# Attention weights spread by transfers instead of matmuls, with a new order of loads

## The chip, the cores and the metric

The kernel runs on one core of one Trainium2 chip. The metric is the device time of one execution in microseconds (us). Three runs of the kernel before took 202.96, 203.83 and 204.58 us; the median, 203.83 us, is the time before.

## What is computed

One transformer layer on x of 2048 rows and 512 columns, in bf16. Attention has 32 heads of 16 columns, and each row attends to 8 rows: itself and the rows 2, 4, ... 14 before it. The feed-forward part (FFN) has 1376 columns and multiplies a ReLU gate with a second projection.

```
qkv = layernorm(x) @ wqkv                    # q, k, v: 32 heads x 16
idx = pos[:, None] - 2 * arange(8)           # 8 rows per position, masked below 0
attn = softmax(einsum("bhsd,bhswd->bhsw", q, k[idx]) * 16**-0.5)
o = einsum("bhsw,bhswd->bhsd", attn, v[idx])
h = x + o @ wo
g = layernorm(h) @ W_gate
out = h + (g * (g > 0) * (layernorm(h) @ W_up)) @ W_down
```

## The kernel before

The rows are worked on in four chunks of 512, numbered 0 to 3 (`tk`). The activations lie transposed: `xnT`, `qT`, `kT`, `vT`, `OT` and `hnT` have 512 columns of the model spread over 128 partitions and 4 slices, and the rows along the free dimension. A chunk passes through these stages, and the engines work on several chunks at a time:

- Layer norm of x. DVE makes the statistics (L419, L422), ACT the reciprocal root (L432, L436), DVE the normed rows (L454, tiles named `row`). PE transposes them (L483) and ACT or DVE copies them out (L499, L497); for two pairs of rows in chunk 3 and for most of h, the transpose is a transfer on SP's queue (L472).
- Projections q, k, v: 12 tiles of four matmuls (L524), each copied out by ACT (L532). In chunk 0 the first four tiles go in halves of 256 columns.
- Scores. DVE multiplies q with four shifted views of k at a time (L571, 128 x 4096 elements; four such products a chunk), PE sums over the columns of a head (L577), ACT takes the exponential (L593). The 8 weights of a head come in two halves (`hf`) of four, each a tile `ex` of 128 partitions: 4 weights x 32 heads. In chunk 0 DVE masks them (L596). PE sums the weights (L610), ACT makes the reciprocal (L613, L616). In chunks 1 to 3 DVE multiplies the weights with it (L625).
- Spreading. v has four partitions for each head, so each weight's 32 partitions are spread to 128. PE does this with four matmuls against a 0/1 matrix for each half (L638), and ACT copies the four results (L644) into a tile `ab` of 128 x 8 x 512 from the pool `big`.
- Sum over the 8 rows. DVE multiplies `ab` with eight shifted views of v (L659, four products a chunk), and sums by halving (L662, then L666 or L685, which writes `OT`). In chunks 0 to 2 the first halving is an accumulating transfer on POOL's queue (L691).
- Output projection on PE (L711; in chunk 0 the residual is added there too, L714), residual and sums on ACT (L720) or DVE (L722), then the layer norm of h (L400, L408, L429, L436, L454) and its transposes.
- FFN. Up and gate tiles on PE (L749), ACT copies (L753) and ReLU (L756), DVE's product `gT` (L769), the down projection on PE (L786), the residual on DVE (L797), the store on SP's queue (L801).

The order on each engine is written out. Every step is added to a planner with an engine, a duration, a latency and the buffers it takes; a list RANK gives each step its place; the planner walks through the queues of the engines, picks for each the step with the lowest rank, assigns buffers by the planned times, and the instructions are issued in the order of the planned starts. Loads have planned arrival times and no place in a queue: they are issued in `setup()`. On the chip each engine works in the issued order and waits for semaphores.

Eight completion counts serve the transfers that SP and ACT issue, in turn: each transfer waits before its issue until the eighth transfer before it has landed.

The start: the four tiles of x of chunk 0 are loaded in turn from SP and ACT, then four loads of the q and k weights, each a quarter of the rows of both, then x of chunk 1 on SP (L285). The v weights are held back until the first tile of x has landed (L299, L300), and x of chunks 2 and 3 until that of chunk 1 has (L301, L303). wo, the up, gate and down weights follow on SP. PE runs 44 matmuls on zeros meanwhile (L373), and 8 after each of the first two transposes (L381).

Of the kernel before, what the change touches and what calls it, by code (L numbers as in the profile page):

```python
# [18 lines left out]
    0, 1, 2, 3, 4, 5, 6, 7, 8, 9, 10, 11, 12, 13, 14, 15, 16, 18, 19, 24,  # L19
    26, 31, 32, 17, 20, 22, 23, 25, 29, 34, 35, 28, 33, 37, 39, 41, 45, 48, 21, 27,  # L20
    30, 36, 38, 42, 44, 46, 63, 74, 40, 56, 68, 49, 51, 54, 43, 60, 72, 53, 66, 65,
    77, 70, 83, 75, 80, 90, 92, 87, 114, 102, 110, 85, 105, 93, 104, 115, 125, 129, 78, 88,
    95, 99, 103, 183, 193, 202, 132, 143, 150, 156, 152, 106, 109, 116, 123, 119, 168, 181, 216, 220,
    224, 180, 188, 217, 223, 231, 187, 196, 226, 229, 234, 162, 172, 201, 205, 207, 237, 240, 239, 245,
    247, 251, 242, 248, 243, 246, 252, 256, 259, 263, 250, 254, 265, 266, 272, 278, 269, 276, 285, 275,
    283, 273, 280, 286, 318, 322, 292, 301, 304, 314, 313, 324, 341, 311, 325, 298, 303, 334, 338, 326,
    330, 346, 354, 360, 337, 355, 317, 353, 347, 358, 370, 329, 352, 340, 348, 332, 345, 294, 350, 356,
    361, 374, 343, 365, 372, 381, 351, 362, 413, 357, 368, 367, 386, 418, 400, 425, 460, 464, 417, 427,
    457, 467, 376, 434, 446, 466, 410, 429, 437, 668, 55, 61, 52, 57, 50, 58, 47, 59, 62, 64,
    67, 84, 73, 82, 86, 71, 81, 69, 79, 89, 166, 175, 122, 136, 111, 130, 137, 190, 91, 101,  # L30
    127, 173, 149, 179, 94, 96, 163, 213, 158, 170, 98, 107, 108, 167, 208, 197, 249, 257, 244, 235,
    255, 260, 264, 268, 274, 296, 279, 302, 309, 305, 310, 307, 287, 295, 290, 293, 300, 319, 328, 364,
    369, 315, 320, 359, 363, 335, 342, 380, 382, 327, 336, 373, 375, 389, 395, 387, 392, 396, 402, 393,
    399, 398, 401, 397, 403, 405, 409, 404, 407, 411, 412, 416, 419, 420, 423, 421, 428, 422, 426, 431,
    474, 482, 441, 443, 458, 463, 453, 468, 483, 438, 448, 436, 452, 442, 451, 450, 454, 456, 488, 492,
    479, 498, 455, 487, 491, 500, 507, 461, 493, 445, 459, 481, 485, 471, 475, 496, 511, 539, 524, 533,
    520, 535, 526, 530, 541, 514, 540, 484, 502, 543, 544, 556, 581, 589, 538, 552, 559, 562, 549, 554,
    584, 587, 529, 547, 560, 564, 113, 120, 100, 124, 76, 117, 97, 112, 128, 133, 140, 144, 142, 146,
    164, 145, 154, 148, 157, 161, 209, 230, 174, 186, 198, 200, 195, 215, 182, 184, 199, 228, 189, 211,
    169, 177, 178, 194, 232, 241, 271, 281, 185, 191, 261, 253, 284, 297, 289, 282, 308, 312, 321, 331,  # L40
    339, 344, 378, 366, 377, 371, 379, 383, 385, 394, 388, 391, 390, 430, 439, 470, 490, 424, 432, 473,
    476, 440, 447, 486, 489, 406, 415, 465, 477, 501, 518, 497, 504, 508, 512, 494, 499, 521, 525, 517,
    519, 516, 522, 503, 505, 527, 528, 532, 546, 534, 537, 536, 548, 531, 542, 579, 597, 566, 594, 585,
    601, 561, 580, 609, 599, 603, 588, 592, 571, 575, 577, 600, 605, 606, 610, 595, 623, 602, 611, 582,
    614, 627, 558, 576, 574, 578, 568, 572, 565, 567, 583, 621, 648, 639, 645, 636, 649, 591, 616, 652,
    624, 635, 628, 633, 640, 655, 663, 665, 667, 632, 654, 661, 711, 650, 656, 707, 710, 644, 657, 659,
    669, 126, 138, 118, 134, 131, 139, 121, 135, 141, 147, 155, 160, 151, 171, 159, 165, 153, 176, 203,
    236, 218, 225, 192, 204, 214, 219, 258, 291, 262, 270, 222, 233, 267, 277, 227, 238, 212, 221, 288,
    316, 206, 210, 306, 299, 323, 333, 384, 349, 408, 414, 433, 435, 444, 462, 449, 506, 510, 509, 513,
    515, 469, 495, 478, 472, 480, 563, 570, 586, 593, 523, 551, 557, 569, 573, 590, 596, 598, 545, 550,  # L50
    553, 555, 615, 622, 604, 607, 612, 619, 608, 613, 626, 629, 618, 620, 630, 631, 617, 625, 634, 637,
    638, 641, 646, 653, 643, 651, 642, 647, 691, 695, 681, 692, 694, 698, 688, 697, 700, 679, 687, 674,
    677, 670, 680, 666, 671, 690, 673, 675, 672, 682, 658, 662, 660, 678, 683, 684, 689, 664, 685, 699,
    702, 676, 693, 705, 701, 706, 704, 709, 686, 703, 708, 713, 715, 716, 718, 696, 714, 719, 720, 722,
    724, 731, 712, 726, 732, 734, 717, 725, 727, 730, 728, 733, 735, 737, 721, 723, 729, 736,
# [3 lines left out]
class Op:  # L59


    __slots__ = ("eng", "dur", "lat", "fn", "deps", "prio", "take", "use", "start", "done", "seq", "key")

    def __init__(self, eng, dur, fn, deps=(), prio=0.0, take=(), use=(), lat=0.0):
        self.eng, self.dur, self.fn, self.lat = eng, dur, fn, lat
        self.deps = [d for d in deps if d is not None]
        self.prio, self.take, self.use = prio, list(take), list(use)
        self.start = self.done = None
# [23 lines left out]
class Plan:  # L92
# [23 lines left out]
    def order(self):  # L116
# [14 lines left out]
        while left:  # L131
# [36 lines left out]
            op.start, op.done = t, t + op.dur + op.lat  # L168
            free[op.eng] = t + op.dur
# [18 lines left out]
def kernel(  # L188
# [20 lines left out]
    PADL = 16  # L209
    SCALE = DH ** -0.5  # L210
# [45 lines left out]
    big_s = slots(5, [P, W, CS], BF16, "big")  # L256
    gT_s = slots(7, [P, 2, CS], BF16, "gT")
    ex_s = slots(3, [P, CS], BF16, "ex")
    ln_s = slots(1, [P, CS], F32, "lnd")
# [18 lines left out]
    def setup():  # L278
# [4 lines left out]
        for dt in range(NT):  # L283
            (nc.scalar if dt % 2 else nc.sync).dma_start(wqk_sb[:, dt:dt + 1, :], w3_r[:, dt:dt + 1, 0:2 * D])
        nc.sync.dma_start(x_sm[:, BPC:2 * BPC, :], x_rows[:, BPC:2 * BPC, :])  # L285
# [13 lines left out]
        nc.gpsimd.tensor_copy(out=wv_sb[0:1, 0, 0:1], in_=x_sm[0:1, 0, 0:1])  # L299
        nc.sync.dma_start(wv_sb[:], w3_r[:, :, 2 * D:3 * D])  # L300
        nc.gpsimd.tensor_copy(out=x_sm[0:1, 2 * BPC, 0:1], in_=x_sm[0:1, BPC, 0:1])  # L301
        for tk in range(2, NCK):
# [4 lines left out]
        nc.sync.dma_start(wg_sb[:], B_W_gate.rearrange("(dt p) f -> p dt f", p=P))  # L307
        nc.sync.dma_start(
            wd_sb[:, 0:NFF, :], B_W_down[0:NFF * P, :].rearrange("(ft p) n -> p ft n", p=P))
        if FTAIL:  # L310
            nc.sync.dma_start(wd_sb[:FTAIL, NFF, :], B_W_down[NFF * P:F, :])

# [24 lines left out]
    NWARM, NFILL = 44, 8  # L337
    DMAT = (('h',2,0),('h',2,2),('x',3,0),('x',3,2),('h',3,0),('h',3,2),('h',1,0))

    EARLY = (1, 2, 3)  # L340

# [11 lines left out]
    MM, TP = 0.2165, 0.07  # L353
# [8 lines left out]
    def load(t):  # L362
        return add(None, "LD", 0.0, None, lat=t)

    xload = [[load(t) for t in (3.4, 3.4, 4.2, 4.2)]] + [[load(t)] * BPC for t in (9.5, 14.0, 15.5)]
    wload = {n: load(t) for n, t in
             (("q", 8.0), ("k", 8.0), ("v", 12.0), ("o", 17.5), ("u", 21.5), ("g", 25.5), ("d", 29.5))}
# [7 lines left out]
    fills = [add(("warm", 0), "PE", 5.7, f_warm, [], -500, take=[wb])]  # L375
# [9 lines left out]
    def layernorm(tk, src, dst_slots, pr, groups, on_act, residual=None):  # L385
# [7 lines left out]
        for grp in groups:  # L393
# [72 lines left out]
            for j0 in range(lo, hi, step):  # L466
                if (ln, tk, j0) in DMAT:
                    for j in range(j0, min(j0 + step, hi)):
                        xn, a = norm(j)

                        def f_td(j=j, xn=xn):
                            nc.sync.dma_start_transpose(out=dst.t[:, :, j * P:(j + 1) * P], in_=xn.t[:])  # L472

                        evs.append(add((ln + "td" + gk, tk), "SP", TDD, f_td, [a], pr, take=[dst], use=[xn], lat=TDL))
                    continue
# [31 lines left out]
    for tk in range(NCK):  # L507
# [9 lines left out]
        seq = [(c, t) for t in range(NT) for c in (0, 1)] + [(2, t) for t in range(NT)]  # L517
        for n, (c, t) in enumerate(seq):
# [38 lines left out]
        for hf in range(2):  # L557
# [26 lines left out]
            if tk in MERGE:  # L584
                scd = [add(("sc%d" % hf, tk), "PE", 4 * MM + SW, lambda p=prd: [f() for _, _, f in p],
                           [a for a, _, _ in prd], apr, take=[sc], use=[b for _, b, _ in prd], lat=PEL)]
            else:
                for a, pb, f in prd:
                    scd.append(add(("sc%d" % hf, tk), "PE", 2 * MM + SW, f, [a] + scd[-1:], apr,
                                   take=[sc], use=[pb], lat=PEL))  # L590
# [17 lines left out]
        def f_dn(exs=exs, dn=dn, tk=tk):  # L608
# [9 lines left out]
        b = add(("den", tk), "PE", 2 * MM, f_dn, exd, apr + 2, take=[dn], use=exs, lat=PEL)  # L618
# [11 lines left out]
        ab, abd = Buf(big_s), []  # L630
        for w0 in range(0, W, BCN):
            hf = w0 // 4
            bcs = [Buf(at_s) for _ in range(BCN)]
# [17 lines left out]
        for t in range(NT):  # L651
# [35 lines left out]
            for n, du in ((4, D20), (2, D10), (1, D2)):  # L687
                f = lambda n=n, mt=mt, f=f_a: f(n, mt)
                if n == 4 and (tk, t) in DACC:
# [3 lines left out]
                    m = add(("ta%d" % t, tk), "POOL", 1.5, f_da, [m], tpr, use=[mt], lat=DAL)  # L693
# [85 lines left out]
        for n, (j, c0, c1) in enumerate(parts):  # L779
# [20 lines left out]
            def f_os(j=j, c0=c0, c1=c1, ob=ob, tk=tk):  # L800
                nc.sync.dma_start(out_rows[:, tk * BPC + j, c0:c1], ob.t[:, c0:c1])  # L801
# [9 lines left out]
            add(("os%d" % n, tk), "SP", 0.15, f_os, [b], mb + 6, use=[ob], lat=2.0)  # L811
# [42 lines left out]
```

## Time and profile before

| | |
|---|---|
| median of three runs | 203.83 us (202.96 to 204.58) |
| span of the profiled execution (first to last instruction) | 200.7 us |
| that execution's own time | not listed by the page; the median lies 3.1 us above the span |
| PE busy | 193.4 us (96%) |
| DVE busy | 153.3 us (76%) |
| ACT busy | 121.8 us (61%) |
| transfers | 18.81 MB, mean 94 GB/s |
| first projection, first FFN tile, last down projection ends | 7.96, 65.22, 197.17 us |

Busy times are sums over the instructions of an engine. The strip of 40 digits divides the span into equal slices of 5 us and gives the busy share of each in tenths. A line of the waits names who waited, for whom, the sum in us, how often, and the longest. A line of the chain gives the start, the length and the work; "issue" is time in which the engine waited for nothing the profile shows. A line of the timeline gives start and length; the bracket at its end says how long the engine stood idle before it and what ended that. A line of the groups gives the busy time, the mean of one instruction in ns and the idle time before them. A line of the transfers gives their number, the size of each and the median time from issue to landing.

### The profile page before, as it was taken

How to read it: one execution, taken by the hardware profiler on the slowest of the kernel's cores; microseconds unless marked ns; L12 is line 12 of the kernel's file. 1: busy time of each engine (PE TensorE's matmuls, PEld its weight loads, DVE VectorE, ACT ScalarE, POOL GpSimd, SP SyncE). 2: the span in 40 equal slices, each digit the busy share in tenths (PEclk: the TensorE clock that was granted, in tenths of full speed). 3: DMA queues.
4: the chain of work that ended last, by engine and by line, in shares of the span. 5: the costliest groups of instructions: out<-in, count | busy, mean ns of one | idle time of the engine just before them, and what ended most of it. 6: DMA issues, size and time to landing. Idle time of an engine off the chain costs nothing.

```text
span 200.7 us, 2938 instructions
## 1 busy us (share of the span) xinstructions
PE 193.4 (96%) x1095; PEld 96.2 (48%) x1115; DVE 153.3 (76%) x239; ACT 121.8 (61%) x256; POOL 12.7 (6%) x28
## 2 busy tenths in 40 slices
PE   8999999989999999999999999999999999999992
PEld 8776445445445344444444444444444444444451
DVE  6989998989999999999996868799967412022313
ACT  3576798747899965887436779701566631277400
POOL 4000000410000013100131000000000000000000
PEclk9999999999999999999999999999999999999999
DMA  6989933994000009920399400131010050200103
GB/s 204 322 245 409 388 119 66 170 201 87 3 0 0 3 0 183 195 40 3 57 178 193 124 3 0 29 75 52 3 52 0 0 104 3 78 0 0 52 0 105
DMA packets 17676, 18.81 MB, mean 94 GB/s; under 512 B 8352, under 2 KB 14464, under 8 KB 17664
## 3 DMA queue, kind: packets, MB, share of 16 engines
q1 hardware_dynamic: 15360, 11.57, 18.5%
q0 software_dynamic: 1728, 6.29, 16.6%
q10 hardware_dynamic: 576, 0.79, 1.2%
q8 instruction: 8, 0.13, 0.3%
q14 instruction: 4, 0.03, 0.0%
HBM read 8.42 MB, written 2.10 MB: 52 GB/s over the span
## 4 chain that ended last, share of the span: by engine, by line
PE 67%; DVE 16%; DMA 6%; ACT 5%; issue 2%; SPq 1%; ACTq 0%
PE bank L749 29%; PE bank L524 15%; PE bank L786 14%; DVE big L659 6%; PE bank L711 5%; DMA quad<-row 5%; DVE big L571 3%; DVE gT L769 2%; DMA x_sm<-in_A_x_dram 1%; SPq L472 1%; PE bank L483 1%; DVE x_sm L722 1%; DVE big L662 1%; DVE row L454 1%; PE bank L577 1%
## 5 line engine op out<-in xcount | busy, mean ns | idle before, releaser
L749 PE MATMUL bank<-quad,wu_sb 128*128 128x512 bf16 (+1 forms) x172 | 42.4, 379 | 0.4
L749 PE MATMUL bank<-quad,wg_sb 128*128 128x512 bf16 (+1 forms) x173 | 42.0, 379 | 0.4 <-DMA quad<-row 0.3
L756 ACT ACTIVATE gr<-bank 128x512 bf16<-128x512 f32 (+1 forms) x44 | 25.3, 616 | 24.7 <-PE bank L749 22.9
L786 PE MATMUL bank<-wd_sb,gT 128*128 128x512 bf16 (+2 forms) x183 | 39.8, 366 | 0.2
L753 ACT CAST up_sb<-bank 128x512 bf16<-128x512 f32 (+1 forms) x44 | 25.0, 600 | 21.0 <-PE bank L749 17.3
L571 DVE TENSOR_TENSOR big<-quad,kT 128x4096 bf16<-128x4096 bf16 x16 | 36.2, 2284 | 0.2
L659 DVE TENSOR_TENSOR big<-big,vT 128x4096 bf16<-128x4096 bf16 x16 | 35.9, 2281 | 0.0
L769 DVE TENSOR_TENSOR gT<-gr,up_sb 128x1024 bf16<-128x1024 bf16 (+1 forms) x24 | 15.3, 642 | 24.0 <-ACT up_sb L753 14.4
L524 PE MATMUL bank<-quad,wqk_sb 128*128 128x512 bf16 (+1 forms) x139 | 29.9, 355 | 1.0 <-DMA quad<-row 0.8
L786 PEld LDWEIGHTS <-gT 128*128 128x128 bf16 (+1 forms) x187 | 18.1, 98 | 19.7 <-issue 0.4
L749 PEld LDWEIGHTS <-wg_sb 128*128 128x128 bf16 (+1 forms) x176 | 17.3, 100 | 21.2 <-issue 0.9
L749 PEld LDWEIGHTS <-wu_sb 128*128 128x128 bf16 (+1 forms) x176 | 17.5, 100 | 20.6 <-issue 0.7
L524 PEld LDWEIGHTS <-wqk_sb 128*128 128x128 bf16 x144 | 15.6, 114 | 12.8 <-issue 2.3
L797 DVE TENSOR_TENSOR row<-x_sm,bank 128x512 bf16<-128x512 bf16 (+1 forms) x17 | 10.6, 649 | 10.4 <-PE bank L786 10.4
L644 ACT CAST big<-bank 128x512 bf16<-128x512 f32 x32 | 17.8, 635 | 0.4 <-PE bank L638 0.2
L662 DVE TENSOR_TENSOR big<-big 128x1024 bf16<-128x1024 bf16 (+2 forms) x24 | 16.8, 728 | 0.1
L691 POOL DMA_DIRECT2D big<-big x12 | 10.5, 873 | 88.1 <-DVE big L659 59.9
L524 PE MATMUL bank<-quad,wv_sb 128*128 128x512 bf16 x62 | 15.6, 380 | 0.2
L711 PE MATMUL bank<-wo_sb,quad 128*128 128x512 bf16 x62 | 15.2, 379 | 0.2
L454 DVE TENSOR_SCALAR row<-x_sm,mv,rs 128x512 bf16<-128x512 bf16 x32 | 11.4, 407 | 3.7 <-ACT rs L436 3.1
L532 ACT CAST quad<-bank 128x512 bf16<-128x512 f32 x16 | 9.5, 612 | 4.6 <-PE bank L524 4.6
L499 ACT COPY quad<-bank 128x1024 bf16<-128x1024 bf16 (+1 forms) x9 | 8.0, 929 | 6.0 <-PE bank L483 6.0
(68 smaller groups left out, 147.2 us busy)
## 6 DMA issues: line engine op xcount, KB each, us to landing
big<-big POOLq DMA_DIRECT2D x12, 512.0 KB, 5.6
out_dram<-row SPq DMA_DIRECT2D x15, 128.0 KB, 1.8
x_sm<-in_A_x_dram SPq DMA_DIRECT2D x3, 512.0 KB, 5.5
wu_sb<-in_B_W_up_dram SPq DMA_DIRECT2D x1, 1376.0 KB, 8.6
wg_sb<-in_B_W_gate_dram SPq DMA_DIRECT2D x1, 1376.0 KB, 11.6
wd_sb<-in_B_W_down_dram SPq DMA_DIRECT2D x1, 1280.0 KB, 14.9
wqk_sb<-in_A_wqkv_dram ACTq DMA_DIRECT2D x2, 256.0 KB, 5.0
wqk_sb<-in_A_wqkv_dram SPq DMA_DIRECT2D x2, 256.0 KB, 5.2
```

Of the source, the lines that this page charges most:

```text
L454: V.tensor_scalar(out=xn.t[:], in0=x, scalar1=mv.t[:, j, 0:1], scalar2=rs.t[:, j:j + 1], op0=ALU.add if residual else ALU.subtract, op1=AL ...
L524: nc.tensor.matmul(mm.t[:, lo:hi], lhsT=wv_sb[:, dt, t:D:NT] if c == 2 else wqk_sb[:, dt, c * D + t:(c + 1) * D:NT], rhs=xnT.t[:, dt, lo:h ...
L571: V.tensor_tensor(out=pb.t[:].rearrange("p (t w) s -> p t w s", t=2), in0=q4, in1=k4, op=ALU.mult)
L644: nc.scalar.copy(out=ab.t[:, w, :], in_=bc.t[:])
L659: V.tensor_tensor(out=mt.t[:], in0=ab.t[:], in1=v8, op=ALU.mult)
L662: V.tensor_tensor(out=mt.t[:, 0:n, :], in0=mt.t[:, 0:n, :], in1=mt.t[:, n:2 * n, :], op=ALU.add)
L711: nc.tensor.matmul(od.t[:], lhsT=OT.t[:, t, j * P:(j + 1) * P], rhs=wo_sb[:, t, :], start=(t == 0), stop=(t == NT - 1 and tk not in RPE))
L749: nc.tensor.matmul(mm.t[:fs, :], lhsT=w_sb[:, dt, ft * P: ft * P + fs], rhs=hnT.t[:, dt, :], start=(dt == 0), stop=(dt == NT - 1))
L753: nc.scalar.copy(out=ub.t[:fs, i, :], in_=um.t[:fs, :])
L756: nc.scalar.activation(out=gr.t[:fs, i, :], in_=gm.t[:fs, :], func=ACT.Relu)
L769: V.tensor_tensor(out=gt.t[:fs, 0:n, :], in0=gr.t[:fs, 0:n, :], in1=ub.t[:fs, 0:n, :], op=ALU.mult)
L786: nc.tensor.matmul(od.t[:, c0:c1], lhsT=gts[ft].t[:fs, ft % 2, j * P:(j + 1) * P], rhs=wd_sb[:fs, ft, c0:c1], start=(ft == 0), stop=(ft == ...
```

## The change

- `ab` gets a buffer of its own, and the pool `big` has four instead of five. All spreading matmuls L638 and copies L644 go. In their place SP issues, for each half, four transfers within SBUF, one for each weight: 32 partitions of `ex` are read four times each and written to the 128 partitions of `ab[:, w, :]`, 128 KB each, 32 in all.
- The q weights are loaded first (two loads, on SP and ACT), then the k weights (two), then x of chunk 1 in two halves, one on SP and one on ACT, ahead of ACT's table load. The v weights wait for the first q load instead of the first x tile. In chunk 0 the projections go in the order q, k, v instead of q and k in turn.
- The loads of the gate and down weights become steps of the planner. In SP's order they stand where they stood.
- 42 warm-up matmuls instead of 44, and 4 instead of 8 after each of the two transposes.
- The last of the 17 stores in the planner's list is issued by ACT instead of SP.
- The planner models a queue of transfers (`dq`), some of its durations change, and RANK is a new list, so the order changes on every engine. On DVE, chunk 0's first normed row stands ahead of the third L419; three L419 of chunk 2 stand ahead of chunk 1's normed rows; five instead of four products L571 stand between chunk 0's last `OT` slice and the normed rows of h; chunk 1's first product with v stands after two instead of four products of later scores.
- Three switches are added that are off (`PRE`, `DEN1`) or change no instruction.

```
-    big_s = slots(5, [P, W, CS], BF16, "big")
+    NAB = 1
+    big_s = slots(5 - NAB, [P, W, CS], BF16, "big")
+    ab_s = slots(NAB, [P, W, CS], BF16, "ab") if NAB else big_s
...
-        for dt in range(NT):
-            (nc.scalar if dt % 2 else nc.sync).dma_start(wqk_sb[:, dt:dt + 1, :], w3_r[:, dt:dt + 1, 0:2 * D])
-        nc.sync.dma_start(x_sm[:, BPC:2 * BPC, :], x_rows[:, BPC:2 * BPC, :])
+        for c in range(2):
+            for h in range(2):
+                (nc.scalar if h else nc.sync).dma_start(
+                    wqk_sb[:, 2 * h:2 * h + 2, c * D:(c + 1) * D], w3_r[:, 2 * h:2 * h + 2, c * D:(c + 1) * D])
+        for h in range(2):
+            j = BPC + 2 * h
+            (nc.scalar if h else nc.sync).dma_start(x_sm[:, j:j + 2, :], x_rows[:, j:j + 2, :])
         nc.scalar.preload_act_table_set("natural_log_exp_and_others")
...
-        nc.gpsimd.tensor_copy(out=wv_sb[0:1, 0, 0:1], in_=x_sm[0:1, 0, 0:1])
+        nc.gpsimd.tensor_copy(out=wv_sb[0:1, 0, 0:1], in_=wqk_sb[0:1, 0, 0:1])
         nc.sync.dma_start(wv_sb[:], w3_r[:, :, 2 * D:3 * D])
...
-    NWARM, NFILL = 44, 8
+    NWARM, NFILL = 42, 4
...
+    BCD = tuple((k, h) for k in range(4) for h in range(2))
+    DMI = 0.42
...
+        if tk == 0:
+            seq = [(c, t) for c in range(3) for t in range(NT)]
...
-        ab, abd = Buf(big_s), []
+        ab, abd = Buf(ab_s), []
         for w0 in range(0, W, BCN):
             hf = w0 // 4
+            if (tk, hf) in BCD:
+                def f_bd(w0=w0, ab=ab, ex=exs[hf]):
+                    for w in range(w0, w0 + 4):
+                        r = w % 4 * HB
+                        nc.sync.dma_start(ab.t[:, w, :], ex.t[r:r + HB, :].unsqueeze(1).to_broadcast([HB, 4, CS]))
+
+                abd.append(add(("bd%d" % hf, tk), "SP", 4 * DMI, f_bd, [exd[hf]], apr + 1, take=[ab],
+                               use=[exs[hf]], lat=0.7, dq=(0.2, 1.54 - 3 * DMI)))
+                continue
...
-            def f_os(j=j, c0=c0, c1=c1, ob=ob, tk=tk):
-                nc.sync.dma_start(out_rows[:, tk * BPC + j, c0:c1], ob.t[:, c0:c1])
+            last = tk == NCK - 1 and n == len(parts) - 1
+
+            def f_os(j=j, c0=c0, c1=c1, ob=ob, tk=tk, q=nc.scalar if last else nc.sync):
+                q.dma_start(out_rows[:, tk * BPC + j, c0:c1], ob.t[:, c0:c1])
```

## Prediction

> **What bounds the kernel now.** I read the busy times first, then who waited for whom, then the chain of work that ended last, and last the timeline of the start.
>
> ```profile
> PE 193.4 (96%) x1095; PEld 96.2 (48%) x1115; DVE 153.3 (76%) x239; ACT 121.8 (61%) x256; POOL 12.7 (6%) x28
> ...
> PE   8999999989999999999999999999999999999992
> ...
> DVE  6989998989999999999996868799967412022313
> ```
>
> ```profile
> PE bank L373 <- DVE warm L287: 1.0, 1, 1.0
> PE bank L524 <- DMA quad<-row: 0.8, 1, 0.8
> PE bank L483 <- DVE row L454: 0.5, 1, 0.5
> PE bank L749 <- DMA quad<-row: 0.3, 1, 0.3
> ```
>
> PE sets the end: after 7.96 us it waits twice, 1.1 us in all. DVE is as full as PE up to about 105 us and half idle after it. So work taken from PE shortens the span only while DVE (and the transfers that DVE hands over) delivers in time in the first half.
>
> ```profile
> 23.55 0.33 PE bank L638 x4
> ...
> 34.86 5.65 DMA quad<-row
> 40.51 0.14 issue
> 40.64 5.99 PE bank L524 x27
> ```
>
> ```profile
> L644 ACT CAST big<-bank 128x512 bf16<-128x512 f32 x32 | 17.8, 635 | 0.4 <-PE bank L638 0.2
> ...
> L638 PE MATMUL bank<-ex,spread 32*128 32x512 bf16 x32 | 3.2, 384 | 0.0
> ```
>
> The chain prices one group of four spreading matmuls at 0.33 us of PE. The groups show what hangs on them: 32 copies on ACT.
>
> ```profile
> 2.60 1.28 ACT L286 ACT_TABLE_LOAD   x1 [2.60 <-issue]
> ...
> 3.50 0.39 SPq L285 DMA_DIRECT2D x_sm<-in_A_x_dram  x1
> ...
> 4.71 0.30 ACT L432 ACTIVATE rs<-mv,eps_t 128x1 f32<-128x1 f32 x1 [0.82 <-DVE mv L422]
> ...
> 7.42 0.39 DVE L497 COPY quad<-bank 128x512 bf16<-128x512 bf16 x1
> ...
> 7.96 0.60 PE L524 MATMUL bank<-quad,wqk_sb 128*128 128x256 bf16 x4
> ```
>
> PE's first useful projection starts 0.15 us after the DVE copy L497; the warm-up matmuls ahead of it only fill.
>
> ```profile
> big<-big POOLq DMA_DIRECT2D x12, 512.0 KB, 5.6
> out_dram<-row SPq DMA_DIRECT2D x15, 128.0 KB, 1.8
> ```
>
> These two rows are the nearest to the new transfers.
>
> **The change part by part.** The page gives the profiled execution only its span, 200.7 us; the three runs have a median of 203.83 us, 3.1 more, and I carry that 3.1 over unchanged.
>
> *Spreading matmuls and copies out.* 8 groups x 0.33 = 2.64 us leave PE. The 32 copies (about 0.49 us from one to the next) leave ACT. ACT's longest waits are for PE (22.9 and 17.3 us), so this is worth nothing by itself. Term: -2.64.
>
> *Spreading transfers in.* 32 transfers of 128 KB on SP, four for each half of a chunk. A store of the same size (128 rows of 1 KB) takes 0.39 us to issue and lands 1.8 us after its issue, so four land 3 x 0.39 + 1.8 = 3.0 us after the first issue: the lower end. The upper end is the accumulating SBUF transfer, 5.6 us for 512 KB. I take 3.0, because size, queue and kind of descriptor are the store's.
> Chunk 0: between the second mask L596 and the first product L659 DVE now has three L422 and eight L454, 3.1 us, as cover. DVE reaches that product at about 32.3 us (31.77 before, plus the late start below), and the second half has landed at about 32. It is hidden with nearly nothing to spare.
> Chunk 1: the second L625 is followed by two L571 (2 x 2.2 us) before the first L659; with the first half's issues ahead of it, landing leaves 0.8 us to spare. L659 also comes two L571 earlier than before.
> Chunks 2 and 3 have 3 us and more. Term: 0; ends 0 and +4.4 (worked out with the rivals). The one weights buffer is free in time: the last L659 of a chunk lies at least 1 us before the next chunk's first transfer.
> Behind these issues on SP stand the four transposes of chunk 3's x. The eight issues end at about 30.6 us (before, the transposes started at 30.89), so these are not later.
>
> [...] The source of each transfer is 32 partitions. [...] No row of the trace reads 32 partitions.
>
> *Start.* The second half of chunk 1's x is now the fifth transfer on ACT's queue, ahead of the table load. The fifth on SP (L285) started only at 3.50, when the first x load had landed, and the same wait stands before ACT's. So ACT issues at 3.50 to 3.95, loads its table to 5.23, and the first L432 starts 0.5 us later than 4.71. DVE then does L454 at 5.8 (now ahead of the third L419), L419 0.62, L454 0.34, L422 0.17, L419 0.62, L422 0.17, and L497 starts at 8.1: PE starts q at about 8.55 instead of 7.96. q and k come in the same 1 MB as before; before, PE did not wait for them. The ten warm-up matmuls fewer (2 x 0.11 + 8 x 0.056 = 0.7 us) stood in front of this point and bring nothing. Term: +0.6; ends 0 (DVE's new order makes it good) and +1.0.
>
> *Chunk 3's x.* PE reaches those tiles at about 39.8 + 0.6 - 2.4 = 38.0 us: two groups (0.66) and two tiles (8 matmuls of 0.216 us, 1.7) less stand before. The last transpose is issued at 34.3; uncontended ones land in 2.5 us, before it took 5.65 beside the accumulations. It now starts ahead of the first accumulation. Wait 0.4 instead of 0.8. Term: -0.4; ends -0.8 and +2.
>
> *First FFN tile.* Counting DVE's new order: four L659 from 32.3 to 41.2, two L571 (4.4) and four trees (L662 0.6 and 0.36, L666 0.34: 5.2) to 50.9 (before 51.27), then five L571 instead of four before the L454 of h, 11.2 us, so these run with one L625 from 62.1 to 63.8 (before 60.83 to 62.15). PE transposes and ACT copies follow, and the first FFN tile can start at 65.2. PE would be there at 65.2 + 0.6 - 0.4 - 3 x 0.33 = 64.4. Term: +0.8; ends 0 and +2.
>
> *Chunk 1's output.* From 63.8 DVE has one L625 and two L571 (4.7), then four L659 (8.8), two L571 (4.4), four L769 (2.4), two L625 (0.7) and four short trees (3.8): OT is complete at 88.7 (before 90.04). PE, three groups lighter by then, wants it at 88.6. But chunk 2's transfers are issued at 82 to 85 us beside the last accumulation, which the tree needs at 87.7 and which takes 5.6 us even alone. Term: +0.6; ends 0 and +2.
>
> *Chunk 1's h.* Its L454 come about 0.8 us earlier, and its two transposes now run between two accumulations. The 0.3 us wait goes. Term: -0.3; ends -0.3 and +1.
>
> *Weights g and d* are issued in the same place of SP's queue, with no wait added: 0. The v load waits for q (about 5.9 us), is still 8 us ahead of its use: 0. Later chunks are bound by PE, whose remaining work is counted above.
>
> *Last store.* At the end SP issues seven stores in order; the last had to stand 0.4 us behind the one before it. One goes to ACT, which is idle. Term: -0.3; ends -0.4 and 0.
>
> Sum: -2.64 + 0.6 - 0.4 + 0.8 + 0.6 - 0.3 - 0.3 = -1.64. The pieces of 0.05 us of issue around the removed groups, some 0.2, go too: -1.8. Forecast 203.8 - 1.8 = 202.0.
>
> **Rivals.**
> Full gain: DVE keeps up and no new wait appears. Then only -2.64 + 0.6 - 0.8 - 0.3 - 0.3 = -3.4 remains, 200.4. For it: ACT is free of 17.8 us, and that was what the chain followed from 56 to 68 us. Against: DVE has no idle time to make up the late start.
> Swallowed gain: DVE is the bound of the first half, and every group taken from PE before 105 us (six, 2.0 us) comes back as a wait of PE. Then -0.66 - 0.3 + 0.6 = -0.4 is left, 203.4. For it: DVE's nines up to 105 us. Against: chunk 1's products are reached earlier.
> Late landing, the one that ends slower: the four transfers land later than 3.0 us. Each us more moves the L659 of chunk 0, all of DVE and the first FFN tile by one; in chunk 1 what exceeds 0.8 us comes on top. The gain of 1.8 is gone at about 4.3 us a half. At the upper end, 5.6, it is 2.6 + 1.8 = 4.4: 206.4, slower by over 1%.
> Cold PE: less fill between 5.6 and 8.5 us lets PE's clock fall. Warm-ups took 0.110 us each at first, 0.056 in the fill, so projections of q at half speed for 3 us would cost 1.5: 203.5. [...]
>
> **How the numbers follow.** A measurement of this kernel can tell about 1%, 2.0 us, from no change. Forecast 0.40 (half of it beyond 1%), full gain 0.22, swallowed 0.18, late landing 0.16, cold PE 0.04. Faster by over 1%: 0.22 + 0.22 = 0.44. Slower by over 1%: most of late landing with its collisions, 0.14. Within: 0.42. The range reaches from somewhat under the full gain (all start terms at their good ends) to late landing at 5.2 us (2.2 + 1.4 - 1.8 = +1.8): 199.6 to 205.6.
>
> **What would show it.** PE without L638 and ACT without L644; first projection at 8.5 us and ACT's table load at 4 us; L659 of chunk 0 at 32.3 us with no DVE wait for a transfer; first FFN tile at about 65 us; PE's waits about 2 us more in sum. A DVE wait for "DMA big" or "DMA ab" ahead of L659 in chunk 0 or 1 would make it late landing; a PE wait on transposes near 38 us beyond 2 us, or a second FFN chunk later than 103.7 us, would make the forecast wrong.

## The result and the profile after

Four runs of the changed kernel took 210.34 to 211.53 us, median 210.97; four of the kernel before 202.96 to 204.58, median 203.7. The ratio is 1.0364 (95% interval 1.0324 to 1.0405): slower by 7.2 us, where the prediction had 1.8 us faster. The profiled execution took 211.53 us with a span of 209.7 us, 9.0 above the span before; it is the slowest of its four, so the two profiles show 1.8 us more than the medians. Its own time lies 1.8 us above its span, where the prediction carried over 3.1. Ratios here and below leave disturbed runs out.

First the page's busy times and strips:

```profile
PE 193.2 (92%) x1054; PEld 95.6 (46%) x1073; DVE 152.4 (73%) x239; ACT 107.4 (51%) x224; POOL 12.7 (6%) x28
...
PE   8699999699599896999979999799999999999993
...
DVE  6697994899999959995999966999984210160522
...
PEclk9879999999999999999999999999999999999999
```

PE's busy time is the same, though 2.6 us of spreading matmuls and 0.7 us of warm-ups are gone from it. The strip of the granted clock gives one reason: slices 2 and 3 ran slower, and 3.41 us at half clock hold 1.7 us less work. The rest is not accounted for. What grew is the rest of the span: 209.7 - 193.2 = 16.5 us instead of 7.3. PE is still the engine that ends last, but no longer full. Its four largest waits, and DVE's ahead of the products with v:

```profile
PE bank L600 <- DVE big L594: 2.3, 2, 1.7
PE bank L547 <- ACT kT L555: 2.1, 1, 2.1
PE bank L547 <- DMA quad<-row: 2.0, 1, 2.0
PE bank L504 <- DVE row L475: 1.9, 4, 0.7
```

```profile
DVE big L717 <- DMA ab<-ex: 7.9, 3, 3.4
DVE big L717 <- DMA out_dram<-row: 2.5, 1, 2.5
```

Without the wait of 1.0 us ahead of the first warm-up, which both have, PE's listed waits summed to 1.6 us before and sum to 11.1 now. DVE, which waited for no transfer ahead of its products with v (L717; L659 before), waits four times, once in each chunk. The line that names `out_dram` is chunk 3's: it ends at 127.75 us, just after the last spread transfer has landed (127.63) and before the first of the stores lands (127.97), so no store held it.

The timeline of SP around chunk 0's wait, PE's wait for the transposes behind it, chunk 0's first product before, then the products after that wait, and the rows of the transfers:

```profile
28.63 6.57 SPq L686 DMA_DIRECT2D ab<-ex  x8
35.30 5.24 SPq L493 DMA_TRANSPOSE quad<-row  x4
```

```profile
41.89 8.80 PE L547 MATMUL bank<-quad,wqk_sb 128*128 128x512 bf16 x40 [1.99 <-DMA quad<-row]
```

```profile
31.77 2.29 DVE L659 TENSOR_TENSOR big<-big,vT 128x4096 bf16<-128x4096 bf16 x1
```

```profile
37.45 8.90 DVE L717 TENSOR_TENSOR big<-ab,vT 128x4096 bf16<-128x4096 bf16 x4 [3.36 <-DMA ab<-ex]
...
77.02 2.29 DVE L717 TENSOR_TENSOR big<-ab,vT 128x4096 bf16<-128x4096 bf16 x1 [2.13 <-DMA ab<-ex]
...
99.73 2.29 DVE L717 TENSOR_TENSOR big<-ab,vT 128x4096 bf16<-128x4096 bf16 x1 [2.45 <-DMA ab<-ex]
...
127.75 4.50 DVE L717 TENSOR_TENSOR big<-ab,vT 128x4096 bf16<-128x4096 bf16 x2 [2.49 <-DMA out_dram<-row]
```

```profile
big<-big POOLq DMA_DIRECT2D x12, 512.0 KB, 5.1
ab<-ex SPq DMA_DIRECT2D x32, 128.0 KB, 2.7
out_dram<-row SPq DMA_DIRECT2D x15, 128.0 KB, 1.8
```

Chunk 0's eight issues were predicted to end at 30.6 us; they end at 35.2. The transpose transfers behind them start at 35.30 instead of 30.89, so PE waits 2.0 us, until 41.89, for chunk 3's x (0.8 us, until 40.64, before). DVE arrives at its first product at 34.09, 2.3 us later than before, and then waits 3.36. Every later stage carries it: wo of chunk 0 starts at 57.32 (51.87 before), the first FFN tile at 71.70 (65.22), the second chunk's FFN at 112.03 (103.67).

And the start, by windows of 1 us: length, then busy time and count of PE, PEld, DVE, ACT and POOL, the granted clock, the transfers' share and GB/s:

```profile
8.00:9.00 1.00, 0.27 (x1) 0.11 (x1) 1.00 (x4) 0.50 (x2) 0.00 (x0) 1.00 0.55 190
9.00:10.00 1.00, 0.92 (x8) 0.86 (x9) 0.09 (x1) 0.00 (x0) 0.00 (x0) 0.70 0.78 169
10.00:11.00 1.00, 1.00 (x8) 0.73 (x7) 0.49 (x1) 0.00 (x0) 0.18 (x1) 0.50 1.02 354
11.00:12.00 1.00, 1.00 (x8) 0.75 (x6) 1.00 (x3) 0.58 (x1) 0.00 (x0) 0.50 0.50 109
12.00:13.00 1.00, 1.00 (x8) 0.74 (x6) 1.00 (x3) 0.00 (x0) 0.00 (x0) 0.59 1.01 358
```

The clock is 0.50 from 9.4 to 12.8 us. Before, it was 1.00 there. (This fall belongs to the execution as much as to the kernel: of the seven kept profiles of kernels in the new order with this start, four have it and three have not, those of the unspread transfers, of the two queues and of the transfers halved in chunks 2 and 3.) So two of the rivals, late landing and cold PE, stand in this profile side by side. Which of them costs the 7.2 us, the experiments tell.

### The profile page after: what moved, and what is told of

Same layout as the page of the kernel before. It is cut to its first block, busy times and chain, and to the rows that moved or that the text cites. A ratio compares the mean times of both kernels' runs of the same rounds, so it can differ in the third digit from the quotient of the medians.

```text
span 209.7 us, 2905 instructions
## 1 busy us (share of the span) xinstructions
PE 193.2 (92%) x1054; PEld 95.6 (46%) x1073; DVE 152.4 (73%) x239; ACT 107.4 (51%) x224; POOL 12.7 (6%) x28
## 4 chain that ended last, share of the span: by engine, by line
PE 49%; DVE 26%; DMA 8%; SPq 5%; issue 5%; ACT 5%; DVEq 0%; ACTq 0%
PE bank L807 22%; PE bank L844 15%; DVE big L717 9%; PE bank L547 8%; DVE big L594 6%; SPq L686 5%; DMA ab<-ex 4%; DMA wqk_sb<-in_A_wqkv_dram 3%; DVE big L720 3%; DVE gT L827 2%; DVE x_sm L780 2%; PE bank L769 2%; ACT row L429 1%; DVE row L475 1%; PE bank L504 1%
## 5 line engine op out<-in xcount | busy, mean ns | idle before, releaser
L717 DVE TENSOR_TENSOR big<-ab,vT 128x4096 bf16<-128x4096 bf16 x16 | 36.1, 2285 | 10.4 <-DMA ab<-ex 7.9
L844 PE MATMUL bank<-wd_sb,gT 128*128 128x512 bf16 (+2 forms) x182 | 39.0, 366 | 1.2 <-DVE gT L827 0.9
L547 PE MATMUL bank<-quad,wqk_sb 128*128 128x512 bf16 (+1 forms) x141 | 31.4, 368 | 5.2 <-ACT kT L555 2.1
L811 ACT CAST up_sb<-bank 128x512 bf16<-128x512 f32 (+1 forms) x44 | 24.5, 592 | 7.6 <-PE bank L807 5.5
L547 PEld LDWEIGHTS <-wqk_sb 128*128 128x128 bf16 x144 | 16.2, 117 | 18.1 <-issue 6.5
L555 ACT CAST kT<-bank 128x512 bf16<-128x512 f32 x16 | 9.5, 599 | 10.6 <-PE bank L547 5.9
L429 ACT ACTIVATE row<-x_sm,mv 128x512 bf16<-128x512 bf16 x12 | 8.5, 712 | 8.9 <-DVE mv L421 8.9
L440 DVE BATCH_NORM_STATS2 st<-x_sm 128x6 f32<-128x512 bf16 x16 | 10.5, 681 | 2.0 <-DMA x_sm<-in_A_x_dram 2.0
## 6 DMA issues: line engine op xcount, KB each, us to landing
wg_sb<-in_B_W_gate_dram SPq DMA_DIRECT2D x1, 1376.0 KB, 12.8
```

Source lines behind the costliest of these rows:

```text
L547: nc.tensor.matmul(mm.t[:, lo:hi], lhsT=wv_sb[:, dt, t:D:NT] if c == 2 else wqk_sb[:, dt, c * D + t:(c + 1) * D:NT], rhs=xnT.t[:, dt, lo:h ...
L717: V.tensor_tensor(out=mt.t[:], in0=ab.t[:], in1=v8, op=ALU.mult)
L811: nc.scalar.copy(out=ub.t[:fs, i, :], in_=um.t[:fs, :])
L844: nc.tensor.matmul(od.t[:, c0:c1], lhsT=gts[ft].t[:fs, ft % 2, j * P:(j + 1) * P], rhs=wd_sb[:fs, ft, c0:c1], start=(ft == 0), stop=(ft == ...
```

## Experiments: the transfers

**Half the transfers.** The cost that is suspected is halved in all chunks, then in two at a time.

```
-                    for w in range(w0, w0 + 4):
+                    for w in range(w0, w0 + 2):
...
+        nc.gpsimd.memset(ab_s.tiles[0][:], 0.0)
```

> The changed kernel with two of the four spread transfers of each half, 16 instead of 32; the other four slices of the weights buffer are set to zero once at the start, so half of the weights are left out of the sum. A half lands after 0.65 + 2.7 = 3.35 us, the four of chunk 0 after 4.7 instead of 8.8. Theory A (late landing costs what DVE waits): the waits for ab fall from 7.9 us to under 2, chunk 0's first product with v comes about 3 us earlier, at 34.4, the first FFN tile at 68.5 to 69; time 207 to 208.5. Theory B (the order costs, landings are beside the path): over 210.

Measured: ratio 1.0001 (0.9962 to 1.0039). DVE's waits for the transfers fall from 10.4 to 1.5 us, and 7.4 us come back, more than theory A had. PE's wait of 2.0 us for chunk 3's x goes with them, so what a late landing costs DVE and what it costs the transposes behind it are not told apart here. The timeline of DVE shows the waits of chunks 1 and 2 gone:

```profile
35.38 8.90 DVE L718 TENSOR_TENSOR big<-ab,vT 128x4096 bf16<-128x4096 bf16 x4 [1.53 <-DMA ab<-ex]
...
72.75 2.28 DVE L718 TENSOR_TENSOR big<-ab,vT 128x4096 bf16<-128x4096 bf16 x1
...
92.97 2.29 DVE L718 TENSOR_TENSOR big<-ab,vT 128x4096 bf16<-128x4096 bf16 x1
```

The late start is still in this kernel, and the half clock too in its profile (8.4 to 11.9 us). It is level with the kernel before and not faster: the 2.6 us of matmuls that are gone do not show, and no run says what takes them.

```
-                    for w in range(w0, w0 + 4):
+                    for w in range(w0, w0 + k):
```

with k = 2 in chunks 0 and 1 and 4 in the others, then the other way round:

> The changed kernel with two of the four transfers of each half in chunks 0 and 1 (half of their weights left out of the sum), all four in chunks 2 and 3. With this in all chunks 7.3 us came back. Theory A (every DVE wait up to 105 us costs its length): the waits of chunk 0 and 1 fall from 5.5 to 1.5 us, that of chunk 2 stays at 2.5: 4 to 5 us come back, 206 to 207. Theory B (only the first FFN tile decides, as the prediction had it; chunk 2's wait is beside PE's work): nearly all 7.3 comes back, 203.5 to 204.5.

Measured: 1.0221 (1.0168 to 1.0274), 2.9 us back, less than either theory had. Chunk 2's wait stays:

```profile
98.49 2.29 DVE L718 TENSOR_TENSOR big<-ab,vT 128x4096 bf16<-128x4096 bf16 x1 [2.60 <-DMA ab<-ex]
```

> The other side of the same cut: two of four transfers in chunks 2 and 3 alone (half of their weights left out). Theory A: chunk 2's wait of 2.5 us goes, and as much of the time: 208 to 209. Theory B: under 1 us, 210 to 211.

Measured: 1.0231 (1.0180 to 1.0281), 2.7 us back, as theory A had it. Chunk 2's product now starts without a wait, at 97.63 instead of 99.73:

```profile
97.63 2.29 DVE L718 TENSOR_TENSOR big<-ab,vT 128x4096 bf16<-128x4096 bf16 x1
```

Chunk 3's wait is gone as well. So the landings of chunks 2 and 3, which the prediction had 3 us and more to spare, cost about 2.7 us together; the first FFN tile is not the only place that decides. How much of it is chunk 2's alone was not tested. The two cuts sum to 5.6 of the 7.4 us; the difference is within what the intervals leave open.

**What makes a transfer slow.** The same bytes from all partitions, unspread:

```
-                        nc.sync.dma_start(ab.t[:, w, :], ex.t[r:r + HB, :].unsqueeze(1).to_broadcast([HB, 4, CS]))
+                        nc.sync.dma_start(ab.t[:, w, :], ex.t[:])
```

> The changed kernel with every spread transfer read from all 128 partitions of the weights tile instead of 32 partitions four times each: same number, size, queue and order, but the weights are not spread, so the attention it computes is another one. Theory A1 (the narrow source makes the transfer slow): issue 0.40 us and landing 1.8 us as in the store row, a half after 3.0 us, the eight of chunk 0 after 5 us instead of 8.8; DVE's waits for ab fall from 7.9 us to under 3, and the time to 207 to 209. Theory A2 (any 128 KB transfer within SBUF is that slow, or the queue is shared with the loads): issue 0.60, landing 2.7, waits and time as in the changed kernel, 210.5 to 211.5.

Measured: 1.0194 (1.0131 to 1.0258). The row of the transfers:

```profile
ab<-ex SPq DMA_DIRECT2D x32, 128.0 KB, 2.1
```

Between the two theories: the narrow source is 0.6 us of the landing, and those 0.6 us, with the waits that they end, are worth 3.5 us of the kernel's time. The issue is 0.60 us here as well, so this transfer within SBUF takes longer to issue than the store (0.39) with either source, and its landing does not come down to 1.8 us.

Two queues:

```
-                        nc.sync.dma_start(ab.t[:, w, :], ex.t[r:r + HB, :].unsqueeze(1).to_broadcast([HB, 4, CS]))
+                        (nc.scalar if w % 2 else nc.sync).dma_start(ab.t[:, w, :], ex.t[r:r + HB, :].unsqueeze(1).to_broadcast([HB, 4, CS]))
```

> The changed kernel with the second and fourth spread transfer of each half issued by ACT instead of SP. If the issue at 0.6 to 0.8 us on one queue sets the landing, a half lands about 1.2 us sooner and the eight of chunk 0 about 3 us sooner, DVE's waits for ab (10.4 us with the one put down to out_dram) fall to about 5, and the time to 207 to 209, less what ACT loses by waiting for DVE ahead of its issues. If the transfer engines set it (the plain source of the same bytes was only half as much better), landing grows as issue shrinks and the time is 210 to 213.

Measured: 1.0267 (1.0224 to 1.0311), 2.0 us back. DVE's idle time ahead of its products halves, as expected, from 10.4 to 5.2 us, but the time stays above the 207 to 209 us that were expected with it. The landings in the rows:

```profile
ab<-ex SPq DMA_DIRECT2D x16, 128.0 KB, 4.4
ab<-ex ACTq DMA_DIRECT2D x16, 128.0 KB, 4.9
```

With two queues the issues overlap and the landings stretch from 2.7 to 4.4 and 4.9 us. One queue is part of the limit, the transfers themselves are the other: in the changed kernel they move 194 to 203 GB/s from 31 to 34 us, 0.65 us for 128 KB, with one after another.

Set side by side: that idle time fell from 10.4 us to 6.6 (halved in chunks 0 and 1), 5.8 (in 2 and 3), 6.5 (unspread) and 1.5 (halved in all), and 2.9, 2.7, 3.5 and 7.4 us of time came back.

**The matmuls back, in the new order.**

```
-    BCD = tuple((k, h) for k in range(4) for h in range(2))
+    BCD = ()
```

> The changed kernel with the spreading done by PE and ACT again (32 matmuls, 32 copies, in the ranks that the transfers had; the buffer for the weights stays apart), loads and warm-ups as changed. Theory A: DVE's waits for ab, 7.9 us, and most of the 2.5 put down to out_dram go; PE gets 2.6 us of matmuls back. Start stays late. 206 to 208. Theory B: DVE finds the next wait at once, and PE has 2.6 us more to do: 210 to 213.

Measured: 1.0781 (1.0726 to 1.0836), slower still by 8.5 us, outside both theories. The profile points to the edit itself: a transfer waits on SP's queue, where little stands behind it; a matmul in the same rank waits on PE, with all of PE's work behind it (L705 waits 4.8 us for ACT copies, and the clock is 0.50 from 74.2 to 81.0 us). It says nothing about the cost of the transfers. It does say that matmuls can't simply take the transfers' places in this order. What the new order costs by itself, with the spreading as before, stays untested.

## Experiments: the start and the clock

> The changed kernel with the loads of the kernel before: q and k weights together in four quarters of their rows, x of chunk 1 in one load on SP, the v weights held for the first x tile. Theory A: ACT's table load starts at 2.6 us instead of 4.0, PE's first projection at 8.0 instead of 9.1, x of chunk 1 is there at 9.1 instead of 10.5, and PE has no gap at 8 to 9 us, so that the clock may hold too: the first score product 1.5 to 3.5 us earlier, 207.5 to 209.5. Theory B: within 0.5 us of 211.0.

```
+        for dt in range(NT):
+            (nc.scalar if dt % 2 else nc.sync).dma_start(wqk_sb[:, dt:dt + 1, :], w3_r[:, dt:dt + 1, 0:2 * D])
+        nc.sync.dma_start(x_sm[:, BPC:2 * BPC, :], x_rows[:, BPC:2 * BPC, :])
...
+        nc.gpsimd.tensor_copy(out=wv_sb[0:1, 0, 0:1], in_=x_sm[0:1, 0, 0:1])
```

The lines of the change that they replace go. Measured: 1.0312 (1.0257 to 1.0367), 1.0 us back, about as little as the intervals can tell. The clock is 1.00 at the start of its profile (and falls once at 40.8 us). DVE arrives at chunk 0's product at 32.16 instead of 34.09, then waits 3.55 instead of 3.36.

The opposite edit, in the kernel before, with the warm-ups:

```
-    NWARM, NFILL = 44, 8
+    NWARM, NFILL = 42, 4
...
+        for h in range(2):
+            j = BPC + 2 * h
+            (nc.scalar if h else nc.sync).dma_start(x_sm[:, j:j + 2, :], x_rows[:, j:j + 2, :])
```

> The kernel before with the new loads (q weights first, then k, then x of chunk 1 in halves on SP and ACT ahead of the table load; v weights held for q) and the new warm-ups (42 and 4); everything else as before, spreading by matmul. Theory A (the start costs by itself): ACT's table load at 4.0 us, q at 9 us and x of chunk 1 at 10.5, a clock of 0.50 for about 3.5 us after 9 us; the first score product 2 to 3.5 us later than 14.52, and the time 205.5 to 207. Theory B (DVE and PE make a late start good by 65 us): 203.5 to 205.

Measured: 1.0008 (0.9973 to 1.0044). In the order of before no cost of the new start shows: the first product with v starts at 32.38 instead of 31.77, 0.6 us late as the prediction had it, and that is made good. The clock stayed at 1.00 in its profile.

```profile
32.38 8.89 DVE L663 TENSOR_TENSOR big<-big,vT 128x4096 bf16<-128x4096 bf16 x4
```

The two edits of half the transfers and of the old loads together:

> The changed kernel with two of the four transfers of each half (16 instead of 32, half of the weights left out of the sum) and the loads of the kernel before; warm-ups as changed (42 and 4). With half the transfers alone the kernel was level with the kernel before. Theory A (what was left of the loss there is the late start): another 1 to 2.5 us, 201.3 to 202.7, which is what the removed matmuls were to give. Theory B (the start is made good by 65 us anyway): 203.2 to 204.

Measured: 1.0000 (0.9966 to 1.0035), as with half the transfers alone. So the start costs about 1 us at most: theory B held twice, and nearly in the first of the three runs. Cold PE at the start does not explain the 7.2 us.

```
-    NWARM, NFILL = 42, 4
+    NWARM, NFILL = 44, 8
```

> The changed kernel with the warm-ups of the kernel before: 44 at the start and 8 after each of the first two transposes. Theory A (the loss of 7.2 us is the sum of a late, cold start, 3.7 us at the first score product, and of spread transfers that land late, waits of 7.9 us on DVE): the granted clock stays at 1.00 from 9 to 13 us instead of 0.50, the first score product comes 1 to 1.8 us before 18.18, and the time falls by as much, to 209.2 to 210. If the ten matmuls (0.7 us) are too few to hold the clock, nothing changes. Theory B (the new order of DVE and PE is what costs, clock and landings are beside the path): the clock may recover, the time stays within 0.5 us of 211.0.

Measured: 1.0504 (1.0438 to 1.0570), not faster but slower by 2.8 us, which neither theory had. The profiled execution is the fastest of its four (211.03 us), so the loss is hardly in the profile. Its clock is 1.00 up to 41.8 us, and then falls twice, after waits of 2.3 and 2.1 us. The windows about the first, busy times as above:

```profile
38.40:41.81 3.41, 1.07 (x6) 0.41 (x5) 3.41 (x3) 0.68 (x2) 1.01 (x1) 1.00 0.48 97
41.81:45.23 3.42, 3.42 (x9) 1.18 (x8) 3.42 (x2) 1.56 (x3) 1.72 (x2) 0.50 1.03 195
45.23:46.00 0.77, 0.77 (x5) 0.37 (x4) 0.77 (x2) 0.00 (x0) 0.00 (x0) 1.00 1.13 213
```

> The changed kernel with the loads and the warm-ups of the kernel before (44 and 8), and more warm-ups in PE's two longest waits: 30 ahead of chunk 3's first projection and 24 ahead of chunk 3's first score sum. With the loads alone the profiled run had one stretch of clock 0.50 (40.9 to 44.4 us, after a wait of 2.16 us), with the warm-ups alone two (41.9 to 45.2 after 2.3 us, 82.7 to 86.3 after 2.1 us). Theory C (each such wait costs a second time, 3.5 us at half clock, 1.8 us): the clock stays at 1.00 all through, and the time is 1.8 us or more under 210.5, with less scatter: 206.5 to 208.5. If the clock is off the path: 209 to 210.5.

The added lines put the warm-ups ahead of the two steps:

```
+        def f_fill(o=o, n=n, f=o.fn):
+            for _ in range(n):
+                nc.tensor.matmul(o.take[0].t[:, 0:P], lhsT=warm[:], rhs=warm[:], start=True, stop=True)
+            f()
```

Measured: 1.0441 (1.0366 to 1.0516). Both ranges were missed. The clock stays at 1.00 in the two places, and falls elsewhere (54.2 to 57.6 us, after a wait of 2.12). Filling waits of PE with dummy work bought nothing. This interval overlaps that of the changed kernel; why the kernel with the warm-ups alone is slower than the changed one stays open.

## Experiments: the transfers in the order of before

The transfers replace the matmuls and copies in single chunks, and nothing else is moved.

```
+            if tk in SPC:
...
+                    nc.sync.dma_start(ab.t[:, w, :], ex.t[r:r + HB, :].unsqueeze(1).to_broadcast([HB, 4, CS]))
```

with SPC = (0, 1, 3), then (0,), then (3,). With all four chunks the planner is a buffer short, so chunk 2 keeps its matmuls.

> The kernel before with the transfers in place of the matmuls and copies in chunks 0, 1 and 3; order of all other steps, loads and warm-ups as before, chunk 2 by matmul. PE loses 2.0 us of work. Theory A: a half lands 4.65 us after its first issue, not 3.0, and two halves close together after 7.2 or more; DVE waits at its first product with v of chunk 0 and of chunk 1, 2 to 3 us each, which more than cancels the 2 us: 205 to 208. Theory B: transfers are hidden or cost no more than they save: 202 to 204.

Measured: 1.0037 (0.9999 to 1.0074). DVE waits 3.8 us in two chunks:

```profile
34.13 8.90 DVE L675 TENSOR_TENSOR big<-big,vT 128x4096 bf16<-128x4096 bf16 x4 [2.06 <-DMA big<-ex]
...
74.85 8.89 DVE L675 TENSOR_TENSOR big<-big,vT 128x4096 bf16<-128x4096 bf16 x4 [1.75 <-DMA big<-ex]
```

But with 2.0 us less on PE the balance is 0.8 us, not 2 or more: both theories missed, A probably by overrating what a wait of DVE costs in an order that leaves PE other work (argued, not tested).

> The kernel before with spread transfers in chunk 0 alone. With chunks 0, 1 and 3 DVE waited 2.1 us for chunk 0's and 1.8 us for chunk 1's, and the ratio was 1.0037. Theory A (a DVE wait in the first half costs its length, less 0.66 us of matmuls): a ratio of 1.004 to 1.008. Theory B (a wait in chunk 0 is made good later): 0.997 to 1.002.

Measured: 1.0026 (1.0000 to 1.0051), between the two: a wait of 2.1 us, 0.66 us of matmuls saved, some 0.5 us lost.

```profile
34.41 8.90 DVE L675 TENSOR_TENSOR big<-big,vT 128x4096 bf16<-128x4096 bf16 x4 [2.10 <-DMA big<-ex]
```

> The kernel before with spread transfers in chunk 3 and nothing else. With the last store moved as well the ratio was 0.9893, with the last store alone 0.9997. Theory A (the transfers of chunk 3 give it, where DVE is half idle): a ratio of 0.987 to 0.995, 1 to 2.6 us, of which 0.66 us are the removed matmuls. Theory B (the 0.9893 was a matter of the two together, or chance): 0.996 to 1.002.

Measured: 0.9948 (0.9930 to 0.9967). DVE does not wait for a transfer in chunk 3; 1.05 us come, where the removed matmuls account for 0.66.

The last store alone, and then with chunk 3's transfers:

```
-                nc.sync.dma_start(out_rows[:, tk * BPC + j, c0:c1], ob.t[:, c0:c1])
+                q.dma_start(out_rows[:, tk * BPC + j, c0:c1], ob.t[:, c0:c1])
```

> The kernel before with the last store on ACT's queue and nothing else. With this and spread transfers in chunk 3 together the time fell by 1.1%, 2.2 us, where 1 us at most was expected. Theory A (the prediction's term): the store gives 0.3 us, 203.4, and chunk 3's transfers the rest (0.66 us of matmuls, and ACT copies that stood in PE's way). Theory B: the end of the kernel waits for that store longer than counted, and the store gives 1 us or more: under 202.7.

Measured: 0.9997 (0.9968 to 1.0025). No gain of the last store on ACT's queue shows; the interval is too wide to exclude the 0.3 us.

> The kernel before with two parts of the change: spread transfers in chunk 3 alone, where DVE is half idle, and the last store on ACT's queue. PE loses 0.66 us of matmuls in chunk 3, the end 0.3 us. If the landing stays hidden there: 202.5 to 203.2, 0.5 to 1 us under the kernel before. If DVE's wait or the issues beside chunk 1's stores cost more: 203.7 to 205.

Measured: 0.9893 (0.9857 to 0.9929), 201.35 us: the fastest version measured, and faster than the 202.5 to 203.2 us expected. Its interval ends just where that of chunk 3 alone begins, yet no gain of the store alone shows; what the two do together is not settled. Chunk 3's products in its timeline, with no wait for a transfer:

```profile
124.64 2.29 DVE L675 TENSOR_TENSOR big<-big,vT 128x4096 bf16<-128x4096 bf16 x1 [0.22 <-issue]
130.03 2.28 DVE L675 TENSOR_TENSOR big<-big,vT 128x4096 bf16<-128x4096 bf16 x1
137.48 2.28 DVE L675 TENSOR_TENSOR big<-big,vT 128x4096 bf16<-128x4096 bf16 x1
```

## Why the prediction was wrong

- **The step that failed: "Spread transfers in. Term: 0."** It took the store's 3 x 0.39 + 1.8 = 3.0 us a half, "because size, queue and kind of descriptor are the store's". Beside no other traffic (chunk 1's first half, 69.53 to 74.21 us) a half lands 4.7 us after its first issue. Issue (0.60), spacing (0.65) and landing (2.7) are all larger than the store's. With a source of 128 partitions instead of 32 the landing falls from 2.7 to 2.1 us and the issue stays at 0.60, so the narrow source is a part of it; what sets the spacing no run shows.
- **The second half was priced almost as if it were alone.** Chunk 0's got 3.0 us and nothing for the first half ahead of it, chunk 1's only 0.6 us for the issues ahead. But in chunk 0 the masks stand at 28.45 and 30.50 us, and in chunk 1 the two L674 at 69.08 and 70.07, so eight transfers go through one queue: first issue to last landing is 8.7 us in chunk 0, 7.2 in chunk 1, 8.8 in chunk 2, beside the accumulation, and 10.9 in chunk 3. "Hidden with nearly nothing to spare" became a wait of 3.36 us, "0.8 us to spare" in chunk 1 one of 2.13, and "3 us and more" in chunks 2 and 3 waits of 2.45 and 2.49. The first FFN tile, forecast at 65.2 us, came at 71.70.
- **The rival had the mechanism, not the size.** Late landing was named, and that it decides from about 4.3 us a half. Its signs came: DVE waits for `DMA ab` in chunks 0 and 1, and the second chunk's FFN at 112.03 us, not by 103.7. Its rule gives 1.65 + 0.85 - 1.8 = +0.7 us at 4.65 us a half (three spacings of 0.65 and a landing of 2.7); measured is +7.2. It priced a half by itself, moved chunks 0 and 1 alone, and left chunks 2 and 3 out. The upper end, 5.6 us a half, was still below what two halves take, so the range ended too low.
- **The start.** +0.6 us is what the loads and warm-ups cost at chunk 0 by themselves (32.38 against 31.77). In the new order it was 2.3 us at the same point, and putting the old loads back brings 1.0 us of time. PE's first q matmul (8.54 us, 8.55 predicted) and ACT's table load (4.00) came as predicted. The q weights landed at 7.6 and 7.8 us, 6.0 and 6.2 after their issue, and PE's second q matmul waits until 9.08, just after k's first load has landed (9.04). The prediction had taken 5.9 us for q and no wait.
- **Warm-ups "bring nothing".** A clock of 0.50 from 9.4 to 12.8 us did come in the profile, as the rival of cold PE had it, with a chance of 0.04. That the ten matmuls are what let it fall is not shown, since three profiles with the same start have no such fall. For the time the term was about right: no cure of the start brought more than about 1 us, and the ten matmuls put back brought a loss.
- **Chunk 3's x: -0.4 predicted, +1.2 came,** because the issues ahead of the transposes ended at 35.2 instead of 30.6. **Last store: -0.3 predicted;** no gain shows, and the interval does not exclude one of 0.3.
- **A slip in the chances:** half of 0.40 is 0.20, so "faster by over 1%" should have been 0.42, not 0.44. It changes nothing above.
- **What was right:** taking the spreading from PE pays where DVE has time: in chunk 3 of the order of before, the removal of 0.66 us of matmuls gave 1.05 us. That the whole 2.64 us can be had is not shown by any run.

Whether little work on PE is what lets its clock fall, as the rival of cold PE has it, the runs do not show. PE was not idle ahead of the falls: it was busy for 1.84 of the 3.41 us ahead of the fall at 9.4 us, and for 1.07 of as many ahead of the one at 41.8 us above. Nor was a fall sure to follow: in the changed kernel the stretch with PE's wait for chunk 3's x, with 1.65 us busy, was followed by none. The two windows of the changed kernel:

```profile
6.00:9.41 3.41, 1.84 (x20) 1.31 (x21) 3.06 (x9) 1.77 (x7) 0.18 (x1) 1.00 0.90 288
...
40.12:43.54 3.42, 1.65 (x8) 0.94 (x9) 3.42 (x2) 0.58 (x2) 1.87 (x2) 1.00 0.71 139
```

## What to carry to other kernels

Price a transfer by a transfer between the same memories and with the same source shape, and then price all that stand in its queue together, from the first issue to the last landing; here a row of another kind, the store's, gave 3.0 us for a half that took 4.7. Before work is moved from a full engine to a queue, look up which engine waits for the landing and how much other work that engine has in hand: here, in the order of before, the same transfers lose 0.5 us in chunk 0, where DVE is full, and gain 1 us in chunk 3, where it is half idle. In the new order half of them cost 7.4 us. Move such work first in the chunk where the waiting engine has slack, and leave the rest.

## What the runs showed of the hardware

- A spread transfer of 128 KB takes 0.60 us to issue and lands after 2.7 us (2.1 from 128 partitions), against 0.39 and 1.8 for a store of the same size. Beside an accumulation on POOL's queue the first landing of chunk 2 took 4.65 us, in chunk 3 one took 7.0. Single issues stretch to 2.3 us. In chunk 0 the seventh takes 1.96, while only 39 GB/s move from 34 to 35 us; what held it is not settled. The trace has a 16 KB packet of instructions, 1.5 us long, from 32.7 us; whether it holds the transfers was not tested.
- PE's clock fell to 0.50 for 3.41 us (with the matmuls back for twice that, 74.2 to 81.0 us). In the 3.41 us ahead of a fall PE was busy for 1.84 us (changed kernel, fall at 9.41 us), 1.26 (old loads, 40.78), 1.07 and 1.32 (warm-ups, 41.81 and 82.78), 1.77 (two queues, 71.41); unspread for 0.76 of 3.40 us (42.20). In the changed kernel a stretch with 1.65 us busy (40.12 to 43.54 us) and one with 1.82 (53.79 to 57.20) were followed by none. The two falls with the warm-ups lie 40.97 us apart, twelve times 3.41. A wait of 2.12 us (old loads, more warm-ups) was followed by a fall; waits of 2.28 and 2.15 us (halved in chunks 2 and 3) and one of 2.62 (two queues, at 54.96 us) were not. So a wait may cost a second time. In the kernel with transfers in chunks 0, 1 and 3, runs with a mean clock of 0.992 took 205.4 and 206.0 us, those at 0.997 and above 203.1 to 204.9; whether the clock or the wait ahead of it makes the difference is not told apart.
